# Attention pooling followed by SoLU on one core: six one-bank tiles for the first batch, nine early x buffers, output weights spread after pooling

## The chip, the cores and the metric

The kernel runs on one NeuronCore of one Trainium2 chip. The metric is the device time of one execution in microseconds, lower is better. The engines are called as the profile calls them: PE is TensorE (PEld its weight load), DVE is VectorE, ACT is ScalarE, POOL is GpSimd, and SP is SyncE, which here issues every DMA. PSUM has 8 banks; one bank holds 512 fp32 values per partition.

## The reference

```python
def mab(q, kv):                                   # scale = 1/sqrt(128)
    s = scale * (q @ kv.transpose(0, 2, 1))
    s = s - s.max(-1, keepdims=True)
    a = np.exp(s)
    a /= a.sum(-1, keepdims=True) + 1e-09
    return a @ kv
h = mab(I, x)          # x: 4 batches of 12608 tokens, 128 wide; I: 32 inducing rows
x = mab(x, h)          # 50432 tokens of 128
...
h = x @ w_in                                      # 128 -> 1024
solu = h * softmax(h)
ln = (solu - mean) / sqrt(var + 1e-06) * g_ln     # over 1024
out = ln @ w_out                                  # 1024 -> 128
```

All of it is fp32. The two weight matrices arrive as 64-bit floats and are turned to fp32 on the chip.

## The kernel before, in words

A batch has 99 tiles of up to 128 tokens (396 in all). The work on a batch has three parts.

- **Pooling, `p1(b, k)`**: nine blocks of up to 12 tiles. A block of x is loaded, each tile is turned by PE (L561) into a PSUM bank, ACT copies it to SBUF (L547), the turned block is stored in DRAM (`xd`, L571), PE makes the scores against the inducing rows (L589), DVE their maximum (L605, L609, with a PE product L614 that shares it between partitions, L623, L630), ACT the exponentials (L639), DVE transposes them (L659), PE multiplies them with x (L665), and DVE adds that to a running sum (L681). After the ninth block `combine` divides (L707 to L712), turns (L714) and copies the pooled rows (`h4`, L716), and multiplies them with `w_in` (L726, copied by ACT in L728).
- **Attention weights, `p2(b, j)`**: for 4, 8 or 12 tiles the turned block comes back from `xd` (L753), PE makes scores against the pooled rows (L768), and DVE, POOL and ACT make the softmax weights (L775 to L795); PE turns these (L804) and ACT copies them (L812).
- **Each tile, `main` and `soft`**: PE multiplies the turned weights with `h4 @ w_in` into the one `h` tile of two banks (L902), DVE reads it out, scaled and with its extreme (L940), into a buffer of the lock `HN`; ACT takes the exponential into a buffer of the lock `EU` (L950), POOL multiplies the two (L954), ACT sums the squares (L965), and DVE transposes in 32x32 blocks into a buffer `vt` that holds four tiles, a group (L978). PE then multiplies the group with the output weights `wc` (L1023) as two streams: stream 0 uses rows 0 to 63 of the array and the tile `op0`, stream 1 rows 64 to 127 and `op1`, 32 steps each. A step is called a beat here. L902 takes one half of the rows, so a beat of the other stream can run beside it. DVE or ACT copies the results (L1045), POOL and ACT normalise (`finish`, L1066 to L1102), SP stores them.

Pooling of batch b+1 runs among the tiles of batch b. For batch 0 there is nothing to run beside: this early phase borrows buffers that later have another use. x comes into `EARLY_X` (five pieces of the buffer `spare` and one `xn`), the turned x into pieces of `vt`, PSUM banks from the two halves of each `op` tile, two `h_e` banks, `pb` and `tr`. `handover` and `handover_op` give them to their later locks when batch 0 is pooled.

The weights are converted by `rounded`: a load (L405), integer operations on DVE (L410 to L419, L428), a copy on ACT (L421) and six multiplications and additions of half a matrix on POOL (L424 to L431). `weights_in` does that for `w_in`; `weights_out` for `w_out`, and then scales by `g_ln` on ACT (L453), subtracts the mean over the 1024 (PE L464, DVE L469) and spreads the result over `wc` with 16 DMAs (L481). No L1023 runs before all 16 have landed (`wc_ready`). While `rounded` runs, the five `eu` buffers and two `hn` buffers serve it.

The order of the instructions on every engine is made at build time by `Planner`. It keeps a clock for each engine, takes the engine whose next operation can start first, and on it, among the operations ready within `SLACK` of that, the one of smallest priority number. Costs, latencies (`AFTER`) and priorities (`PR_*`, `LATE`, `WOUT`) are constants. On the chip each engine then works its list in order. When PE's clock would stand for over `FILL` ns, the planner puts in transposes of the identity (L488). `SWITCH` is what it adds where PE goes from one kind of work to another, and `EAGER` by how much a beat may be planned ahead of its data.

## Time and profile before

| | us |
|---|---|
| median of 3 runs | 1289.62 (1284.67 to 1293.36) |
| the profiled execution | 1285.68 |
| its span | 1283.9 |
| granted PE clock, mean | 0.992 |

The span runs from the first to the last instruction; 1.8 us lie around it. Batch 0's pooled rows are copied (L716) at 52.4, the first tile is multiplied (L902) at 56.4, the first L1023 starts at 80.2, the last POOL multiplication (L954) ends at 1260.3 and the last L1023 at about 1274. Each PE product of fp32 stands in the profile as two records, a transpose as one. A beat of both streams (two products on each half of the rows) is eight records.

| tiles of L954 | from to us | us a tile | PE busy | DVE | ACT | POOL |
|---|---|---|---|---|---|---|
| 1 to 33 | 60.2 to 163.4 | 3.13 | 100.9 of 103 | 92.5 | 92.1 | 90.6 |
| 199 to 231 | 677.5 to 778.0 | 3.04 | 99.3 of 101 | 92.5 | 92.9 | 91.2 |
| 364 to 396 | 1171.7 to 1260.3 | 2.69 | 87.5 of 88 | 82.5 | 85.4 | 86.3 |

The last three rows of such a table (from 987 us on, when batch 3 is pooled) have no pooling beside the tiles. Busy PE is modelled from pipelined products, so a share near 100% doesn't say that it never waits.

### The profile page before, as it was taken

How to read it: one execution, taken by the hardware profiler on the slowest of the kernel's cores; microseconds unless marked ns; L12 is line 12 of the kernel's file. 1: busy time of each engine (PE TensorE's matmuls, PEld its weight loads, DVE VectorE, ACT ScalarE, POOL GpSimd, SP SyncE). 2: the span in 40 equal slices, each digit the busy share in tenths (PEclk: the TensorE clock that was granted, in tenths of full speed). 3: DMA queues.
4: the chain of work that ended last, by engine and by line, in shares of the span. 5: the costliest groups of instructions: out<-in, count | busy, mean ns of one | idle time of the engine just before them, and what ended most of it. 6: DMA issues, size and time to landing. Idle time of an engine off the chain costs nothing.

```text
span 1283.9 us, 75837 instructions
## 1 busy us (share of the span) xinstructions
PE 1246.2 (97%) x34221; PEld 1120.8 (87%) x34221; DVE 1140.8 (89%) x1825; ACT 1140.1 (89%) x2418; POOL 1104.2 (86%) x981
## 2 busy tenths in 40 slices
PE   8899999999999999999999999999999999999996
PEld 6689888889888888889888998888989999999996
DVE  5589989999898989999888999899999999999993
ACT  5489999999889989999789999989988999999993
POOL 2388988889889988988888997978889999999994
PEclk9999999999999999999899999999999999999998
DMA  9652333331232233332133134233021211111111
GB/s 361 188 164 70 111 103 94 93 111 43 77 117 60 78 102 119 103 109 74 28 102 94 43 103 138 91 101 102 21 82 54 58 55 53 54 38 43 29 29 41
DMA packets 118149, 113.46 MB, mean 88 GB/s; under 512 B 76577, under 2 KB 83777, under 8 KB 117697
## 3 DMA queue, kind: packets, MB, share of 16 engines
q1 hardware_dynamic: 117824, 108.62, 27.6%
q8 instruction: 267, 4.37, 1.4%
q14 instruction: 58, 0.47, 0.1%
HBM read 54.30 MB, written 52.18 MB: 83 GB/s over the span
## 4 chain that ended last, share of the span: by engine, by line
PE 70%; DVE 3%; ACT 2%; issue 1%; POOL 1%; POOLq 0%; DVEq 0%; ACTq 0%
PE op L1023 46%; PE h L902 15%; PE tr L561 2%; PE tr L804 2%; PE tr L768 1%; PE pb L665 1%; PE pb L589 1%; ACT sq L965 1%; DVE spare L940 1%; DVE vt L978 1%; ACT eu L950 1%; POOL eu L954 1%; PE pb L726 0%; DVE hn L940 0%; PE pb L614 0%
## 5 line engine op out<-in xcount | busy, mean ns | idle before, releaser
L1023 PE MATMUL op<-wc,vt 32*128 32x129 f32 x25600 | 1007.7, 275 | 12.5 <-issue 8.4
L1023 PEld LDWEIGHTS op<-wc,vt 32*128 32x128 f32 x25600 | 945.4, 185 | 54.3 <-issue 39.8
L902 PE MATMUL h<-hs,aT 32*128 32x128 f32 x6336 | 442.8, 277 | 3.2 <-DVE spare L940 1.2
L902 PEld LDWEIGHTS h<-hs,aT 32*128 32x128 f32 x6336 | 387.9, 187 | 32.1 <-DVE spare L940 6.2
L954 POOL TENSOR_TENSOR eu<-spare,eu 128x1024 f32<-128x1024 f32 x144 | 341.2, 2376 | 33.8 <-ACT eu L950 33.4
L954 POOL TENSOR_TENSOR eu<-hn,eu 128x1024 f32<-128x1024 f32 x140 | 331.8, 2376 | 25.1 <-ACT eu L950 24.3
L978 DVE STREAM_TRANSPOSE vt<-eu 128x1024 f32<-128x1024 f32 x284 | 349.2, 1233 | 1.1 <-POOL eu L954 0.9
L965 ACT ACTIVATE sq<-eu 128x1024 bf16<-128x1024 f32 x284 | 298.9, 1053 | 17.2 <-POOL eu L954 13.7
L940 DVE TENSOR_SCALAR_CACHE_REDUCE hn<-h,rn 128x1024 f32<-128x1024 f32 x198 | 252.1, 1273 | 38.8 <-PE h L902 30.6
L940 DVE TENSOR_SCALAR_CACHE_REDUCE spare<-h,rn 128x1024 f32<-128x1024 f32 x198 | 251.8, 1272 | 37.2 <-PE h L902 28.2
L950 ACT ACTIVATE eu<-hn,nm 128x1024 f32<-128x1024 f32 x140 | 160.3, 1145 | 19.9 <-DVE hn L940 19.0
L950 ACT ACTIVATE eu<-spare,nm 128x1024 f32<-128x1024 f32 x144 | 164.9, 1145 | 10.7 <-DVE spare L940 10.5
L954 POOL TENSOR_TENSOR spare<-hn,spare 128x1024 f32<-128x1024 f32 x58 | 137.5, 2374 | 15.6 <-ACT spare L950 15.5
L954 POOL TENSOR_TENSOR spare<-spare 128x1024 f32<-128x1024 f32 x54 | 128.0, 2373 | 16.9 <-ACT spare L950 16.4
L978 DVE STREAM_TRANSPOSE vt<-spare 128x1024 f32<-128x1024 f32 x112 | 138.2, 1235 | 0.0
L965 ACT ACTIVATE sq<-spare 128x1024 bf16<-128x1024 f32 x112 | 117.7, 1051 | 9.3 <-POOL spare L954 8.3
L1100 ACT ACTIVATE os<-spare,fin 128x128 f32<-128x128 f32 (+1 forms) x276 | 86.9, 391 | 1.5 <-POOL fin L1085 1.2
L950 ACT ACTIVATE spare<-hn,nm 128x1024 f32<-128x1024 f32 x58 | 66.4, 1145 | 6.7 <-DVE hn L940 6.4
L1045 DVE COPY spare<-op 128x258 f32<-128x258 f32 (+1 forms) x123 | 50.2, 416 | 24.6 <-PE op L1023 23.6
L950 ACT ACTIVATE spare<-spare,nm 128x1024 f32<-128x1024 f32 x54 | 61.9, 1146 | 6.5 <-DVE spare L940 6.5
L965 ACT ACTIVATION_READ_ACCUMULATOR sq<-eu 128x1 f32 x284 | 54.2, 191 | 0.0
L561 PE MATMUL tr<-ident,xn 128*128 128x128 f32 x297 | 48.8, 287 | 0.4 <-DMA xn<-in_x_dram 0.4
(180 smaller groups left out, 1028.0 us busy)
## 6 DMA issues: line engine op xcount, KB each, us to landing
out_dram<-os SPq DMA_DIRECT2D x96, 256.0 KB, 2.4
xT<-xd SPq DMA_DIRECT2D x27, 768.0 KB, 4.6
xn<-in_x_dram SPq DMA_DIRECT2D x22, 768.0 KB, 5.4
xd<-xT SPq DMA_DIRECT2D x21, 768.0 KB, 4.3
dl<-dd SPq DMA_DIRECT2D x396, 1.0 KB, 2.4
xd<-vt SPq DMA_DIRECT2D x7, 768.0 KB, 10.6
spare<-in_x_dram SPq DMA_DIRECT2D x5, 768.0 KB, 10.3
xT<-xd SPq DMA_DIRECT2D x5, 512.0 KB, 4.2
```

The costliest lines, as they stand in the source:

```text
L561: nc.tensor.transpose(out=tr[:, (s - c0) * P : (s - c0 + 1) * P], in_=xn[:, s, :], identity=ident)
L589: nc.tensor.matmul(sc[g * M : (g + 1) * M, : nn * M], lhsT=indT, rhs=xT[:, :nn, g * M : (g + 1) * M], start=True, stop=True)
L804: nc.tensor.transpose(out=tr[:h, (q - q0) * P : (q - q0 + 1) * P], in_=a4[:, q * P : q * P + h], identity=ident)
L902: nc.tensor.matmul(hp[:, cols], lhsT=aT[rows, i // 2, :], rhs=hs[rows, cols], start=True, stop=True)
L940: lambda: nc.vector.tensor_scalar(out=hn, in0=hp, scalar1=rn, scalar2=None, op0=ALU.mult, op1=ALU.min, accum_out=nm),
L950: "ACT", 1133, lambda: nc.scalar.activation(e, hn, AF.Exp, bias=nm, scale=-1.0, accum_out=G["S"][:, s : s + 1]), d, rel, srel,
L954: d = yield Op("POOL", 2330, lambda: nc.gpsimd.tensor_tensor(out=e, in0=hn, in1=e, op=ALU.mult), de, prio=t + PR_MU)
L965: "ACT", 1040, lambda: nc.scalar.activation(sq, e, AF.Square, scale=1.0 / 32.0, accum_out=G["qe"][:, s, 0:1]), d,
L978: lambda: nc.vector.transpose(out=G["vtb"][:, : n * FF].rearrange("p (j s t) -> p j s t", j=M, s=n)[:, :, s, :], in_=e.rearrange("p (a f) ...
L1023: nc.tensor.matmul(op[:rows, a - 2 * w, : C + 1], lhsT=vt[q, k, :], rhs=wc[q, k, :], start=(k == 0), stop=(k == JB - 1))
L1045: return lambda: eng(F["raw"][:rows, i0 : i0 + 2, :], op[:rows, :, : C + 1])
L1100: nc.scalar.activation(os[:rows, q, :], raw[:, q, :], AF.Copy, scale=y[:, i0 + q : i0 + q + 1])
```

## The change

The early phase and the constants of the planner are changed; what is computed stays the same.

- The early phase has six PSUM tiles of one bank each (`bank_e`) instead of four halves of `op` tiles and two `h_e` tiles: three for the turns, three (with `pb`) for scores and pooling. The `op` tiles are made afterwards, with `h`, in the space of the six. `handover_op` is gone, and `p2` of batch 0 uses the bank `tr` alone.
- x comes into nine buffers instead of six: two pieces of `wc` come first, then the five of `spare`, then both `xn`. The buffers for the exponentials move to `wc` and the two `os`.
- Since `wc` is borrowed, the column of ones (L474, now behind the pooled blocks) and the 16 spreads wait until batch 0 is pooled. `w_in`'s load goes from priority -18.5 to -10.5, `w_out`'s conversion from -13.5 to -10.5, the steps behind it (`LATE`) from -13 to -9, `combine` of batch 0 from -12 to -28. The mean over 1024 uses the bank `pb` instead of `tr`.
- After the early phase `HN` has one buffer more and `EU` one less. `EAGER` goes from 60 to 0; early PE work is planned without `SWITCH`.
- `SLACK` goes from 0 to 100 on ACT, from 300 to 100 on DVE and from 0 to 200 on POOL; `PR_MU` (POOL's multiplication) from -1 to -2, `PR_TU` (DVE's transpose) from 3 to 4.

New line numbers are within four of the old ones: L902 is L904 in the changed kernel, L940 L942, L954 L956, L1023 L1025, L481 L482.

```diff
-EAGER = 60
+EAGER = 0
-HN_MORE = 3
+HN_MORE = 4
-LATE = -13
-ON_EARLY = 3
+LATE = -9
-PR_MU = -1
+PR_MU = -2
-PR_TU = 3
+PR_TU = 4
-SLACK = {"PE": 100, "ACT": 0, "DVE": 300, "POOL": 0, "SP": 0}
+SLACK = {"PE": 100, "ACT": 100, "DVE": 100, "POOL": 200, "SP": 0}
-WOUT = -13.5
+WOUT = -10.5
+WIN = -10.5
...
-    op_b = [buf([P, 2, 512], f"op{w}", where=psum) for w in range(2)]
-    op_e = [o[:, i, :] for o in op_b for i in range(2)]
-    early_h = tc.tile_pool(name="h_early", bufs=1, space=PSUM, side="right")
-    where = early_h.__enter__()
-    h_e = [buf([P, 512], f"h_e{i}", where=where) for i in range(2)]
+    bank_pool = tc.tile_pool(name="early", bufs=1, space=PSUM, side="right")
+    where = bank_pool.__enter__()
+    bank_e = [buf([P, 512], f"bank_e{i}", where=where) for i in range(6)]
...
-        o = yield Op("POOL", 200, lambda: nc.gpsimd.memset(wc[:, :, C : C + 1], 1.0))
...
-        mp, rel = yield TRB
+        mp, rel = yield PB
...
+        for k in range(NP):
+            yield p1_done[0][k]
+        o = yield Op("POOL", 200, lambda: nc.gpsimd.memset(wc[:, :, C : C + 1], 1.0), [d for e in p1_done[0] for d in e.after])
+        o_end = [o]
...
-                    lambda: nc.sync.dma_start(rows[a * M : (a + 1) * M, :, q, :C], wg[q * M : (q + 1) * M]), d, issue=600, prio=LATE,
+                    lambda: nc.sync.dma_start(rows[a * M : (a + 1) * M, :, q, :C], wg[q * M : (q + 1) * M]), d, o, issue=600, prio=LATE,
...
-    EARLY_X = Lock([spare[:, i * each : (i + 1) * each].rearrange("p (s c) -> p s c", c=C) for i in range(SPARES * FF // each)] + xn_b[:1])
+    wc_flat = wc.rearrange("p j d -> p (j d)")
+    EARLY_X = Lock([f[:, i * each : (i + 1) * each].rearrange("p (s c) -> p s c", c=C) for f, n in ((wc_flat, 2), (spare, SPARES * FF // each)) for i in range(n)] + xn_b)
...
-    EARLY_TR = Lock(op_e[:3])
-    EARLY_PB = Lock([*h_e, pb_b, op_e[3]])
+    EARLY_TR = Lock(bank_e[:3])
+    EARLY_PB = Lock([*bank_e[3:], pb_b])
...
-            spawn(half(slice(k * 512, (k + 1) * 512)), PRIO_P1(b, NP - 1))
+            spawn(half(slice(k * 512, (k + 1) * 512)), PRIO_P1(b, NP - 1) if b else -28)
...
-        bank = EARLY_TR if b == 0 and j < ON_EARLY else TRB
+        bank = TRB
...
+        bank_pool.__exit__(None, None, None)
+        late = pool("late", 1, PSUM, side="right")
+        give(H, buf([P, FF], "h", where=late), *done)
+        for w in range(2):
+            give(OP[w], buf([P, 2, 512], f"op{w}", where=late), *done)
```

What the built lists say of it, at the three places of which the prediction speaks. First POOL, from the attention weights of tile group 0 to the multiplications of the first tiles (`s_*` and `a_*` are the scores and weights of p2; `hn_83` and `hn_85` with 512 columns are halves of `w_out`; rows of 1024 columns are tiles). Before:

```order
L424 TENSOR_TENSOR hn_83<-hn_83,eu 128x512 x2
L426 TENSOR_TENSOR hn_83<-hn_83,eu 128x512 x2
L431 TENSOR_TENSOR hn_83<-hn_83,eu 128x512 x2
L455 MEMSET wc 128x32
L780 TENSOR_TENSOR s_0_88<-s_0_88,mx_89 128x128
L788 COPY a_94<-a_94 128x4x32
L954 TENSOR_TENSOR eu<-hn_81,eu 128x1024
```

and changed:

```order
L782 TENSOR_TENSOR s_0_90<-s_0_90,mx_91 128x128
L790 COPY a_96<-a_96 128x4x32
L423 TENSOR_TENSOR hn_85<-hn_85,eu 128x512
L782 TENSOR_TENSOR s_1_93<-s_1_93,mx_94 128x256
L423 TENSOR_TENSOR hn_85<-hn_85,eu 128x512
L790 COPY a_96<-a_96 128x8x32
L425 TENSOR_TENSOR hn_85<-hn_85,eu 128x512 x2
L956 TENSOR_TENSOR spare<-hn_83,spare 128x1024
L782 TENSOR_TENSOR s_0_90<-s_0_90,mx_91 128x384
L430 TENSOR_TENSOR hn_85<-hn_85,eu 128x512
L790 COPY a_96<-a_96 128x12x32
L430 TENSOR_TENSOR hn_85<-hn_85,eu 128x512
```

The six halves of `w_out` stood ahead of the first attention weights of batch 0 and now stand between them and the tiles.

Second SP, the issues between the last store of turned x and the first loads of batch 1. Before:

```order
L571 DMA xd<-xT 128x896
L450 DMA g_sb<-in_moe_g_ln_dram 128x8x1
L481 DMA wc<-hn_83 32x8x128 x2
L753 DMA xT_87<-xd 128x1024
L481 DMA wc<-hn_83 32x8x128 x9
L753 DMA xT_87<-xd 128x1536
L481 DMA wc<-hn_83 32x8x128 x5
```

and changed:

```order
L573 DMA xd<-xT 128x896
L755 DMA xT_89<-xd 128x1024
L356 DMA xn_70<-in_x_dram 128x3x512
L755 DMA xT_89<-xd 128x1536 x2
L449 DMA g_sb<-in_moe_g_ln_dram 128x8x1
L755 DMA xT_89<-xd 128x1536
L482 DMA wc<-hn_85 32x8x128 x12
L1001 DMA dd_107<-qe_105 128x8
L482 DMA wc<-hn_85 32x8x128 x4
```

The spreads stood ahead of the second and third load for p2 and now stand behind five of them.

Third PE, the rows up to the first beat. Before, seven tiles are multiplied ahead of it, the last four rows of the way being:

```order
L804 MATMUL op_73<-ident,a_94 128x128 x4
L804 MATMUL op_72<-ident,a_94 128x128 x2
L902 MATMUL h<-hs_124,aT_97 128x128 x8
L561 MATMUL tr<-ident,xn_70 128x128 x4
L1023 MATMUL op_72<-wc,vt 128x129 x2
```

and changed, where they are twelve:

```order
L904 MATMUL h<-hs_126,aT_99 128x128 x8
L563 MATMUL tr<-ident,xn_70 128x128 x4
L489 MATMUL pb<-ident 128x128 x11
L904 MATMUL h<-hs_126,aT_99 128x128 x8
L563 MATMUL tr<-ident,xn_70 128x128 x4
L904 MATMUL h<-hs_126,aT_99 128x128 x8
L591 MATMUL pb<-xT,indT 32x384 x4
L904 MATMUL h<-hs_126,aT_99 128x128 x8
L1025 MATMUL op_637<-wc,vt 128x129 x4
```

Five more tiles stand ahead of the first beat. Over the whole list, counted in the same way, the beats from there to the end are 4187 before and 4195 changed (half-filled ones counted whole), POOL's scalings of the output, L1096 and now L1098, are 31 and 43 (ACT's, L1100 and now L1102, four to a group, 276 and 228), and the copies L1045/L1047 are 123 on DVE and 77 on ACT before, 101 and 99 changed.

More of the change, by code (lines that the diff above doesn't have):

```diff
@@ L311, in set_attention_then_solu_kernel @@
     EW = Lock()
-    OS = Lock(bufs(2, [P, GS, C], "os"))
+    os_b = bufs(2, [P, GS, C], "os")
+    OS = Lock()
     ST = Lock([
@@ L439, in weights_in @@
     def weights_in():
-        g = yield from rounded(w_in_sb, w_in.bitcast(U32), conv, None, conv_free, -18.5)
+        g = yield from rounded(w_in_sb, w_in.bitcast(U32), conv, None, conv_free, WIN)
         plan.set(w_in_ready, g)
@@ L473, in weights_out @@
         )
-        give(TRB, mp, d)
+        give(PB, mp, d)
+        for k in range(NP):
+            yield p1_done[0][k]
+        o = yield Op("POOL", 200, lambda: nc.gpsimd.memset(wc[:, :, C : C + 1], 1.0), [d for e in p1_done[0] for d in e.after])
+        o_end = [o]
         rows = wc.rearrange("p (k q) d -> p k q d", q=4)
@@ L561, in turn4 @@
                     nc.tensor.transpose(out=tr[:, (s - c0) * P : (s - c0 + 1) * P], in_=xn[:, s, :], identity=ident)
-            d = yield Op("PE", SWITCH + 108.7 * (c1 - c0), turn4, [d for d, at in xd if at < c1], trel, prio=None if early else RUSH)
+            d = yield Op("PE", (0 if early else SWITCH) + 108.7 * (c1 - c0), turn4, [d for d, at in xd if at < c1], trel, prio=None if early else RUSH)
             spawn(copy(c0, c1, tr, d), PRIO_P1(b, k))
@@ L591, in scores @@
                 )
-        d = yield Op("PE", SWITCH + n * 60, scores, ready, rel, ind_ready.after)
+        d = yield Op("PE", (0 if early else SWITCH) + n * 60, scores, ready, rel, ind_ready.after)
         def free_xT():
@@ L613, in p1 @@
         )
-        d = yield Op("PE", SWITCH + 110, lambda: nc.tensor.matmul(mq, lhsT=fold2, rhs=v["mdiag"], start=True, stop=True), d)
+        d = yield Op("PE", (80 if early else SWITCH) + 110, lambda: nc.tensor.matmul(mq, lhsT=fold2, rhs=v["mdiag"], start=True, stop=True), d)
         first = k == 0
@@ L1139, in set_attention_then_solu_kernel @@
                 starts.setdefault(NT * (b - 1) + int(P1_FROM + P1_STEP * k), []).append((p1(b, k), PRIO_P1(b, k)))
-        starts.setdefault(max(0, NT * (b - 1)), []).append((combine(b), PRIO_P1(b, NP - 1)))
+        starts.setdefault(max(0, NT * (b - 1)), []).append((combine(b), PRIO_P1(b, NP - 1) if b else -28))
         for j in range(len(at_groups[b])):
@@ L1149, in handover @@
             done += d
+        d = yield hw_ready[0]
+        done += d
+        bank_pool.__exit__(None, None, None)
[3 more added lines that the diff above has]
+            give(OP[w], buf([P, 2, 512], f"op{w}", where=late), *done)
+        give(PB, pb_b, *done)
+        for k in range(NP):
             d = yield xd_done[(0, k)]
             done += d
-        d = yield hw_ready[0]
-        done += d
-        early_h.__exit__(None, None, None)
-        give(H, buf([P, FF], "h", where=pool("h", 1, PSUM, side="right")), *done)
-        give(PB, pb_b, *done)
         wide = 4 * FG * (C + 1)
@@ L1166, in handover @@
         give(XT, xT_b, *done)
+        for o in os_b:
+            give(OS, o, *done)
         give(EW, ew_b, *done)
@@ L1169, in handover @@
             give(XN, a, *done)
-    def handover_op():
-        done = []
-        for k in range(NP):
-            d = yield p1_done[0][k]
-            done += d
-        for j in range(ON_EARLY):
-            d = yield aT_of[(0, j)]["all"]
-            done += d
-        for w in range(2):
-            give(OP[w], op_b[w], *done)
     def handover_tr():
@@ L1187, in set_attention_then_solu_kernel @@
     spawn(handover_tr(), -100)
-    spawn(handover_op(), 0)
     spawn(points(), -40)
```

5 lines of the change are left out of this document (2 added, 3 removed).

## Prediction

> **What bounds the kernel now.** I read the page's busy shares, its chain of waits and its groups first, then PE's timeline in the steady part, then all engines' timelines of the first 90 us.
>
> ```profile
> PE 1246.2 (97%) x34221; PEld 1120.8 (87%) x34221; DVE 1140.8 (89%) x1825; ACT 1140.1 (89%) x2418; POOL 1104.2 (86%) x981
> PE 70%; DVE 3%; ACT 2%; issue 1%; POOL 1%; POOLq 0%; DVEq 0%; ACTq 0%
> 602.12 2.08 PE L1023 MATMUL op<-wc,vt 32*128 32x129 f32 x68
> 604.02 0.28 PE L902 MATMUL h<-hs,aT 32*128 32x128 f32 x2
> ```
>
> PE stands on 70% of the chain that ended last, and the other three are busy for 86 to 89%: PE sets the pace, with little room behind it. The two timeline rows give the price of a beat: 68 records start in 604.02 - 602.12 = 1.90 us, so eight take 0.224 us. The 4187 beats behind the first L1023 are 938 us; the rest of that stretch is pooling and attention weights on PE, the turns between kinds of work, and waits.
>
> The early phase, by its marks:
>
> ```profile
> 8.06 1.53 PE L561 MATMUL op<-ident,spare 128*128 128x128 f32 x12
> ...
> 16.52 1.51 PE L561 MATMUL op<-ident,spare 128*128 128x128 f32 x12
> 17.96 0.85 PE L589 MATMUL pb<-vt,indT 128*32 128x384 f32 x8
> 18.74 0.66 PE L561 MATMUL op<-ident,spare 128*128 128x128 f32 x4
> 19.65 0.86 PE L665 MATMUL h_e<-spare,xn 128*32 128x128 f32 x24 [0.26 <-ACT vt L547]
> ...
> 42.36 0.57 PE L589 MATMUL h_e<-xT,indT 128*32 128x224 f32 x8 [0.69 <-ACT xT L547]
> 43.30 2.19 PE L488 MATMUL tr<-ident 128*128 128x128 f32 x18
> 45.55 2.16 PE L488 MATMUL tr<-ident 128*128 128x128 f32 x18
> 20.00:30.00 10.00, 9.26 (x129) 6.20 (x121) 6.88 (x28) 6.80 (x17) 7.45 (x6) 1.00 1.04 398
> 52.40 0.28 DVE L716 COPY h<-h_e 128x128 f32<-128x128 f32 x1
> 56.35 1.16 PE L902 MATMUL h<-hs,aT 32*128 32x128 f32 x16 [0.46 <-ACT aT L812]
> 80.19 1.50 PE L1023 MATMUL op<-wc,vt 32*128 32x129 f32 x42
> ```
>
> Turning a block of 12 tiles takes PE 1.44 us and its scores 0.78; with the sums against x (L665, 0.8 without its overlap) and the small product, about 0.3, a block costs 3.3 us, eight and a quarter blocks 27 us. PE turns from 8.06 us on, which makes 35 us, yet the pooled rows are copied at 52.4. In between stand fillers (x18 twice near the end) while DVE, ACT and the x still to come are waited for; the stretch from 20 to 30 us (busy PE, PEld, DVE, ACT, POOL, then granted clock, DMA share and GB/s) has the DMA engines full at 398 GB/s. From the pooled rows it takes 4 us to the first tile and 28 to the first L1023.
>
> **The change, part by part.** *Pooling earlier.* All x of batch 0 (6.46 MB) is now issued ahead of everything else: at 398 GB/s 16 us, so it has landed by about 20, and PE can go through its blocks without a wait: 8 + 27 = 35 us. Behind the last scores come the chains of the last blocks; before, 42.36 (the last L589) to 52.40 is 10.0 us, of which 3.1 are `w_out`'s mean and subtraction, which are gone from there. But `w_in`'s conversion now sits in the middle of DVE's list of the early phase. I take 46 us for the copy of the pooled rows, between 42 (35 + 10.0 - 3.1) and 52.4 (nothing gained), and 52 for the first tile: 4 as before plus 2, because ACT's copy for it now stands behind the copy of `w_out`, which waits for DVE's first operation on it.
>
> *The output weights later.* Their chain, each link from a row of before:
>
> ```profile
> 31.15 0.72 DVE L410 TENSOR_SCALAR eu<-eu 128x1024 uint32<-128x1024 uint32 x1 [0.46 <-DMA eu<-in_moe_w_out_dram]
> 34.64 1.22 DVE L415 SCALAR_TENSOR_TENSOR eu<-eu 128x1024 uint32<-128x1024 uint32 x1
> 39.07 2.51 POOL L424 TENSOR_TENSOR hn<-hn,eu 128x512 f32<-128x512 f32 x2 [1.00 <-ACT hn L421]
> 47.51 2.45 ACT L453 ACTIVATE hn<-hn,g_sb 128x128 f32<-128x128 f32 x8
> 49.10 2.05 PE L464 MATMUL tr<-hn,ones_mean 128*128 128x128 f32 x16
> 51.26 1.22 DVE L469 TENSOR_TENSOR hn<-tr,hn 128x1024 f32<-128x1024 f32 x1 [1.37 <-PE tr L464]
> 52.51 1.43 SPq L481 DMA_DIRECT2D wc<-hn  x2
> 54.63 5.92 SPq L481 DMA_DIRECT2D wc<-hn  x9
> 61.25 3.40 SPq L481 DMA_DIRECT2D wc<-hn  x5
> wc<-hn SPq DMA_DIRECT2D x16, 128.0 KB, 4.7
> ```
>
> DVE four operations of 0.72 and two of 1.22, 5.3; POOL three pairs of 2.51, 7.5; ACT 2.45, PE 2.0, DVE 1.2, SP 10.75, landing 4.7: 34 us. In the changed list it starts behind the first reciprocal of p2, some 3.5 us behind the pooled rows, at 49.5. Alone it would end at 83.5; that is the lower end. But POOL's six halves stand between p2's operations and the first tile's multiplication, two of L780 and two of L788 (2.5 us) and one L954 (2.4), and one collision is added:
>
> ```profile
> L780 POOL TENSOR_TENSOR s<-s,mx 128x384 f32<-128x384 f32 (+3 forms) x37 | 28.3, 764 | 13.7 <-DVE mx L777 13.7
> L788 POOL COPY a<-a 128x384 f32<-128x384 f32 (+3 forms) x37 | 17.6, 475 | 4.3 <-ACT a L787 4.2
> L954 POOL TENSOR_TENSOR eu<-spare,eu 128x1024 f32<-128x1024 f32 x144 | 341.2, 2376 | 33.8 <-ACT eu L950 33.4
> 49.60 0.29 DVE L712 TENSOR_SCALAR accn<-acc,small 128x128 f32<-128x128 f32 x1
> 633.42 2.33 DVE L712 TENSOR_SCALAR accn<-acc,small 128x128 f32<-128x128 f32 x1
> 633.33 2.35 POOL L954 TENSOR_TENSOR eu<-hn,eu 128x1024 f32<-128x1024 f32 x1 [0.66 <-ACT eu L950]
> ```
>
> The same small operation of DVE takes 0.29 us beside an idle POOL and 2.33 where POOL had begun a multiplication 0.09 us earlier; both end at 635.68. DVE's L427 (the last operation of the conversion, of the same kind) waits for exactly the POOL operation behind which L956 of the first tile stands, so it starts just after that and stands for some 2.3 us, with the second tile's reading, p2's maximum and the two last halves queued behind it. 83.5 + 2.5 + 2.4 + 2.3 = 90.7, of which the shorter first p2 blocks give back some; I take 90 for the first beat, and 94 for the upper end, where ACT's squares and the `dd` issue among the spreads also hold it. So the first beat comes 90 - 80.2 = 9.8 us later (3 to 14).
>
> [...]
>
> *What PE has to do from there.* Twelve tiles are multiplied by then instead of seven, but the beats that follow are 4195 instead of 4187: +1.8 us. Four turns of tiles, a block of scores and one of p2's stand ahead of the first beat instead of behind it: -1.8. The lists hold the same work otherwise, so a later first beat is a later end where PE is the bound. What comes back: three groups lie ready at 90, and PE has no data to wait for in the first tiles. I put 4 us on that, between 0 and 10 (five tiles of lead at about 2 us of beats that need not wait).
>
> *Balance between the engines.* These rows carry it:
>
> ```profile
> L1096 POOL TENSOR_TENSOR os<-spare,fin 128x512 f32<-128x512 f32 (+1 forms) x31 | 32.3, 1043 | 0.3
> L1045 DVE COPY spare<-op 128x258 f32<-128x258 f32 (+1 forms) x123 | 50.2, 416 | 24.6 <-PE op L1023 23.6
> L940 DVE TENSOR_SCALAR_CACHE_REDUCE hn<-h,rn 128x1024 f32<-128x1024 f32 x198 | 252.1, 1273 | 38.8 <-PE h L902 30.6 <-ACT eu L950 3.9 <-ACT fin L1076 1.3
> 677.00:778.00 101.00, 99.32 (x2791) 90.24 (x2794) 92.47 (x139) 92.89 (x194) 91.17 (x86) 1.00 0.28 84
> 1172.00:1260.00 88.00, 87.50 (x2630) 84.72 (x2632) 82.51 (x106) 85.44 (x183) 86.32 (x73) 1.00 0.12 32
> ```
>
> DVE loses 22 copies of 0.42, 9.2 us, on the engine that PE's next `h` waits for; I count 4 of it, since DVE waits for PE at L940 more than PE for DVE. POOL gains 12 scalings of 1.04, 12.5 us. In the middle it has room (91.2 of 101 busy), at the end none (86.3 of 88); three of the twelve lie in the last 99 tiles: +3.
>
> *The rest.* One more `HN` and one less `EU` buffer, the new slacks, priorities and `EAGER` change which of two ready operations goes first, hundreds of times. No row prices that. PE's 1194 us from 80.2 to the end of its last row
>
> ```profile
> 1261.83 12.25 PE L1023 MATMUL op<-wc,vt 32*128 32x129 f32 x382
> ```
>
> at 1274.1 hold 938 of beats and, by the prices above, about 135 of pooling and attention products; the 121 that remain are turns between kinds and waits. An eighth of these either way is 15 us; I take 0. The six banks of their own cost nothing in themselves: what they change is which early instruction waits, and that is in the 46.
>
> The sum: +9.8 + 1.8 - 1.8 - 4 - 4 + 3 = +4.8. On the profiled execution's 1285.7 that is 1290.5; the median of the runs is 3.9 higher, which would make 1294.4. I forecast 1292.
>
> **Rivals.**
> *PE is not the bound but the chain of a tile through DVE, ACT and POOL.* Then the late first beat is made up for (twelve tiles are ready), the first tile's 56.4 - 52 = 4.4 stays a gain and DVE's copies count in full: 1285.7 - 4.4 - 9.2 = 1272, and with an order that gains the whole 15, 1257. For it speaks that DVE, ACT and POOL together leave PE no room in the last third; against it PE's 70% of the chain.
> *POOL becomes the bound.* It takes the twelve scalings on top of a first beat that is late: 1285.7 + 9.8 + 12.5 = 1308. It decides once POOL's idle time in the middle, 10 of 101 us, falls to the 2 of 88 that it has at the end. Against it: the scalings are spread over all batches, one for every 33 tiles.
> *The early phase is no earlier.* The DMA engines run at their limit until 40 us in either list, and `w_in` now lands behind all x, so its conversion may hold the first tile: pooled rows at 52 as now, the first beat at 96, and 1285.7 + 16 - 5 = 1297. Speaks for it the share of 1.04 above; against it that x needs less than half of these 40 us.
> [...]
>
> ```profile
> 60.00:70.00 10.00, 10.00 (x85) 8.41 (x84) 5.10 (x9) 5.01 (x11) 6.99 (x5) 0.73 1.19 224
> ```
>
> **How the numbers follow.** The forecast's case has 0.40, the early phase that is no earlier 0.10: both end within 1%, which is about what a measurement of this kernel can tell from no change (its three runs span 0.7%). The tile chain as the bound has 0.27 and ends faster by over 1%; POOL as the bound has 0.23 and ends slower by over 1%. The likeliest case's own range is 1278 to 1303 (first beat 3 to 14 later, lead 0 to 10, half of the 15 for the order); with the two others, and about a tenth left out on each side, 1264 to 1312.
>
> **What would show it.** Right: the copy of the pooled rows (L718) near 46, the first L904 near 52, the first L1025 near 90 with twelve L904 ahead of it, DVE's second L427 at over 2 us, the time from the first to the last L1025 within 10 us of 1194. Wrong: a first L1025 before 84, or a stretch of L1025 shorter by more than 15 us, which would say that the order or DVE's relief decides and not PE's count of beats; POOL above 95% from 300 to 1000 us would say the second rival.

## The result

The changed kernel takes 1297.38 us in the median of 14 runs (1292.23 to 1305.58), the kernel before 1288.89 (14 runs, 1284.67 to 1293.36): a ratio of 1.0075, 95% interval 1.0057 to 1.0093. That is 9.7 us longer by the ratio (7.3 to 12.0) and 8.5 by the medians. The profiled execution took 1292.23 us, the shortest of the 14, with a span of 1290.4, against 1285.68 and 1283.9 before.

The page's busy shares and granted clock of the changed kernel (most lines stand two further down than before: L902 is L904 here, L1023 is L1025, L954 is L956):

```profile
PE 1254.5 (97%) x34255; PEld 1129.8 (88%) x34255; DVE 1126.9 (87%) x1806; ACT 1133.3 (88%) x2392; POOL 1116.4 (87%) x990
...
PEclk9889999999999999999999999999999999999998
```

DVE lost 14 us of work (9.2 had been counted) and POOL gained 12 (12.5 counted); PE's share is as it was. The two groups that moved, busy time and mean ns behind the bar:

```profile
L1098 POOL TENSOR_TENSOR os<-spare,fin 128x512 f32<-128x512 f32 (+1 forms) x43 | 44.8, 1042 | 2.7
L1047 DVE COPY spare<-op 128x258 f32<-128x258 f32 (+1 forms) x101 | 41.3, 416 | 25.2 <-PE op L1025 24.3
```

The early phase, PE's timeline first (last scores of pooling, second score product of p2, the turn of p2's first weights, first tile, a later tile and the mean of `w_out`, first beat):

```profile
30.63 0.57 PE L591 MATMUL bank_e<-xT,indT 128*32 128x224 f32 x8 [0.21 <-ACT xT L549]
...
49.27 0.64 PE L770 MATMUL tr<-xT,h 128*32 128x256 f32 x8
52.02 0.41 PE L806 MATMUL tr<-ident,a 128*128 128x128 f32 x2 [0.86 <-DVE s L777]
52.89 1.16 PE L904 MATMUL h<-hs,aT 32*128 32x128 f32 x16 [0.46 <-ACT aT L814]
...
69.86 2.08 PE L904 MATMUL h<-hs,aT 32*128 32x128 f32 x16
71.87 3.44 PE L461 MATMUL pb<-hn,ones_mean 128*128 128x128 f32 x16
...
90.17 0.38 PE L1025 MATMUL op<-wc,vt 32*128 32x129 f32 x2
```

DVE in the same stretch: the pooled rows, the rounding of `w_out` with the transpose of p2's second scores (L777) behind it, the second tile's reading (L942), and the last operation of the rounding (L427).

```profile
43.71 0.29 DVE L718 COPY h<-bank_e 128x128 f32<-128x128 f32 x1 [0.58 <-PE bank_e L716]
...
47.25 0.66 DVE L409 TENSOR_SCALAR eu<-eu 128x1024 uint32<-128x1024 uint32 x1
...
50.29 1.22 DVE L415 SCALAR_TENSOR_TENSOR eu<-eu 128x1024 uint32<-128x1024 uint32 x1
51.43 0.44 DVE L777 STREAM_TRANSPOSE s<-tr 128x256 f32<-128x256 f32 x1
...
58.49 1.28 DVE L942 TENSOR_SCALAR_CACHE_REDUCE spare<-h,rn 128x1024 f32<-128x1024 f32 x1 [2.77 <-PE h L904]
...
60.27 1.06 DVE L427 TENSOR_SCALAR eu<-hn 128x1024 f32<-128x1024 int32 x1
```

ACT's copy of `w_out`, POOL's first multiplication beside that L427, and SP's spreads:

```profile
47.95 1.07 ACT L420 ACTIVATE hn<-eu 128x1024 f32<-128x1024 int32 x1 [0.82 <-DVE eu L409]
```

```profile
58.42 2.35 POOL L956 TENSOR_TENSOR spare<-hn,spare 128x1024 f32<-128x1024 f32 x1
```

```profile
76.64 8.67 SPq L482 DMA_DIRECT2D wc<-hn  x12
85.42 0.54 SPq L1001 DMA_DIRECT2D dd<-qe  x1
86.00 2.57 SPq L482 DMA_DIRECT2D wc<-hn  x4
```

Batch 0's scores end 11.7 us earlier than before (30.63 against 42.36), its pooled rows 8.7 (43.71 against 52.40), the first tile 3.5 (52.89 against 56.35), and the first beat comes 10.0 us later (90.17 against 80.19). The early phase gains, and the gain is used up on the way to the first beat. The tiles themselves are not late by then: the twelfth is multiplied at 89.61 in the changed kernel and at 93.06 before. To see where it grows, the start of POOL's 34th multiplication, the time from there to its 298th, and from there to the span's end, in us (one profiled execution each; the experiments stand here too):

| kernel | 34th | to the 298th | to the end |
|---|---|---|---|
| before | 163.4 | 823.9 | 296.6 |
| changed | 168.8 | 822.8 | 298.8 |
| E1 before, detour | 174.2 | 826.9 | 296.3 |
| E2 changed, detour | 176.3 | 827.0 | 299.0 |
| E3 changed, no rounding | 166.4 | 830.0 | 298.6 |
| E4 changed, conversions early | 168.7 | 824.1 | 301.6 |
| E5 changed, no fillers | 168.8 | 824.3 | 298.9 |
| E6 E4 without fillers | 167.2 | 827.2 | 311.1 |
| E7 changed, old constants | 169.4 | 828.3 | 297.3 |
| E8 before, new constants | 171.1 | 825.0 | 303.3 |
| E9 changed, scalings to ACT | 171.4 | 827.6 | 301.5 |
| E10 before, scalings to ACT | 165.1 | 824.7 | 302.1 |
| E11 before, beat 226 | 164.7 | 827.1 | 296.4 |
| E12 changed, early and old constants | 168.4 | 830.1 | 297.7 |

The changed list stands in E2, E3 and E5 too, with edits at its start or end; these four differ by up to 7 us in the middle column and by 0.4 in the last. How much of the 7 is scatter and how much comes from the edits is not told apart. Of the 6.5 us between the two spans, 5.4 stand ahead of the 34th tile, 2.2 behind the 298th, and the -1.1 between them is too small to read.

### The profile page after: what moved, and what is told of

The parts are those of the page before. It is cut to its first block, busy times and chain, and to the rows that moved or that the text cites. A ratio compares the mean times of both kernels' runs of the same rounds, so it can differ in the third digit from the quotient of the medians.

```text
span 1290.4 us, 75904 instructions
## 1 busy us (share of the span) xinstructions
PE 1254.5 (97%) x34255; PEld 1129.8 (88%) x34255; DVE 1126.9 (87%) x1806; ACT 1133.3 (88%) x2392; POOL 1116.4 (87%) x990
## 5 line engine op out<-in xcount | busy, mean ns | idle before, releaser
L1025 PE MATMUL op<-wc,vt 32*128 32x129 f32 (+1 forms) x25600 | 999.3, 274 | 7.7 <-issue 4.9
L1025 PEld LDWEIGHTS op<-wc,vt 32*128 32x128 f32 (+1 forms) x25600 | 935.9, 184 | 45.3 <-issue 34.2
L956 POOL TENSOR_TENSOR eu<-spare,eu 128x1024 f32<-128x1024 f32 x189 | 447.1, 2373 | 31.5 <-ACT eu L952 31.2
L904 PE MATMUL h<-hs,aT 32*128 32x128 f32 x6336 | 443.4, 277 | 6.5 <-DVE spare L942 4.7
L904 PEld LDWEIGHTS h<-hs,aT 32*128 32x128 f32 x6336 | 387.0, 187 | 39.9 <-DVE spare L942 12.1
L980 DVE STREAM_TRANSPOSE vt<-eu 128x1024 f32<-128x1024 f32 x329 | 404.6, 1234 | 14.4 <-POOL eu L956 13.8
L967 ACT ACTIVATE sq<-eu 128x1024 bf16<-128x1024 f32 x329 | 345.6, 1050 | 30.3 <-POOL eu L956 25.9
L956 POOL TENSOR_TENSOR eu<-hn,eu 128x1024 f32<-128x1024 f32 x140 | 331.4, 2372 | 15.8 <-ACT eu L952 15.2
L942 DVE TENSOR_SCALAR_CACHE_REDUCE spare<-h,rn 128x1024 f32<-128x1024 f32 x228 | 289.8, 1271 | 51.3 <-PE h L904 43.7
L942 DVE TENSOR_SCALAR_CACHE_REDUCE hn<-h,rn 128x1024 f32<-128x1024 f32 x168 | 213.1, 1268 | 29.4 <-PE h L904 24.8
L952 ACT ACTIVATE eu<-spare,nm 128x1024 f32<-128x1024 f32 x189 | 216.2, 1144 | 14.3 <-DVE spare L942 13.6
L956 POOL TENSOR_TENSOR spare<-spare 128x1024 f32<-128x1024 f32 x39 | 92.5, 2372 | 7.9 <-ACT spare L952 7.9
L980 DVE STREAM_TRANSPOSE vt<-spare 128x1024 f32<-128x1024 f32 x67 | 82.7, 1235 | 3.4 <-POOL spare L956 3.1
L967 ACT ACTIVATE sq<-spare 128x1024 bf16<-128x1024 f32 x67 | 70.4, 1050 | 5.5 <-POOL spare L956 4.0
L1102 ACT ACTIVATE os<-spare,fin 128x128 f32<-128x128 f32 (+1 forms) x228 | 72.4, 389 | 1.5 <-POOL fin L1087 1.2
L956 POOL TENSOR_TENSOR spare<-hn,spare 128x1024 f32<-128x1024 f32 x28 | 66.5, 2375 | 6.8 <-ACT spare L952 6.8
L1047 DVE COPY spare<-op 128x258 f32<-128x258 f32 (+1 forms) x101 | 41.3, 416 | 25.2 <-PE op L1025 24.3
L1047 ACT COPY spare<-op 128x258 f32<-128x258 f32 (+1 forms) x99 | 35.6, 368 | 21.0 <-PE op L1025 18.4
L549 ACT COPY xT<-tr 128x512 f32<-128x512 f32 (+1 forms) x75 | 42.8, 571 | 6.5 <-PE tr L563 4.4
```

What stands on the lines that cost most here:

```text
L549: lambda: nc.scalar.copy(xT[:, c0:c1, :], tr[:, : (c1 - c0) * P].rearrange("p (s t) -> p s t", t=P)),
L904: nc.tensor.matmul(hp[:, cols], lhsT=aT[rows, i // 2, :], rhs=hs[rows, cols], start=True, stop=True)
L942: lambda: nc.vector.tensor_scalar(out=hn, in0=hp, scalar1=rn, scalar2=None, op0=ALU.mult, op1=ALU.min, accum_out=nm),
L952: "ACT", 1133, lambda: nc.scalar.activation(e, hn, AF.Exp, bias=nm, scale=-1.0, accum_out=G["S"][:, s : s + 1]), d, rel, srel,
L956: d = yield Op("POOL", 2330, lambda: nc.gpsimd.tensor_tensor(out=e, in0=hn, in1=e, op=ALU.mult), de, prio=t + PR_MU)
L967: "ACT", 1040, lambda: nc.scalar.activation(sq, e, AF.Square, scale=1.0 / 32.0, accum_out=G["qe"][:, s, 0:1]), d,
```

## The experiments

Theory 1 is the prediction's: the late first beat passes to the end. Theory 2: the tiles that are ready make up for it, and the loss lies elsewhere. The others are named as they came up.

**E1 and E2: the first beat later.** In both kernels the output weights make a detour on SP; all orders stay.

```diff
+        trip = xd_pool.tile([P, FF], F32, name="trip")
+        def put():
+            if (a, q) == (2, 3):      # E2: (3, 0)
+                nc.sync.dma_start(trip, wg2)
+                nc.sync.dma_start(wg2, trip)
+            nc.sync.dma_start(rows[a * M : (a + 1) * M, :, q, :C], wg[q * M : (q + 1) * M])
```

> The kernel before, with every engine's order left as it is; only SP, before the last five of the sixteen spreads of the output weights, sends them once to DRAM and back (two transfers of 512 KB, which change no value). The first multiplication by the output weights (the first beat, 80.2 us in the kernel before) should come some 9 to 11 us later. Theory 1 (PE's count of beats sets the end, and a first beat that is late stays late): the time rises by 6 to 11 us, ratio 1.005 to 1.009. Theory 2 (the tiles that are ready by then make up for it, and the changed kernel's loss lies elsewhere): at most 2 us, ratio under 1.002.

> The changed kernel with the same detour of the output weights through DRAM, before the last four spreads, all orders as they are. First beat at 99 to 101 us in place of 90.2. Theory 1: another 6 to 11 us on the changed kernel, so 1303 to 1308, ratio to the kernel before 1.011 to 1.016. Theory 2: 1297 to 1299, ratio 1.0065 to 1.009.

SP's rows in E1 and the first beat (L1031 is L1023 of the kernel before):

```profile
61.14 0.44 SPq L480 DMA_DIRECT2D trip<-hn  x1
69.23 0.32 SPq L481 DMA_DIRECT2D hn<-trip  x1
72.92 3.24 SPq L482 DMA_DIRECT2D wc<-hn  x5
```

```profile
89.75 1.50 PE L1031 MATMUL op<-wc,vt 32*128 32x129 f32 x42
```

E1: 9.6 us later, ratio 1.0066 (1.0040 to 1.0092), that is 8.5 us (5.2 to 11.9); the table shows it ahead of the 34th tile, with nothing given back behind. But the detour did not move the first beat alone. SP works its list in order, so the load of x for batch 1 (L357) that stands behind the spreads was issued at 76.21 in place of 64.70, and PE's next turn waited for it, ahead of the tiles. These are the two rows, and 70 to 80 us before and in E1:

```profile
76.21 0.61 SPq L357 DMA_DIRECT2D xn<-in_x_dram  x1
81.30 1.12 PE L569 MATMUL tr<-ident,xn 128*128 128x128 f32 x4 [10.63 <-DMA xn<-in_x_dram]
```

```profile
70.00:80.00 10.00, 9.38 (x102) 7.76 (x100) 9.46 (x18) 7.74 (x16) 7.60 (x8) 1.00 0.49 167
```

```profile
70.00:80.00 10.00, 0.68 (x13) 0.48 (x10) 3.28 (x4) 0.00 (x0) 1.93 (x4) 0.74 0.75 171
```

Each of the four engines stood for 10.6 to 12.6 us in one piece there, which the changed kernel's do not. The weights were not what PE waited for: by the trace the last spread landed at 78.3, 11.5 us ahead of E1's first beat, and in the kernel before at 71.7, 8.5 us ahead. So the expected first beat came, but by luck, on another path. E1 shows that a stop of all four engines at the start is paid at the end. It does not test a first beat that is late while the tiles go on.

E2: first beat at 94.97, 4.8 later than in the changed kernel (9 to 11 had been expected), ratio 1.0136 (1.0099 to 1.0172), that is 7.9 us above the changed kernel's 1.0075 (some 3 to 13 by the two intervals). The 4.8 are not the detour's: the twelfth tile, which stands ahead of the beat, is itself 4.8 late (94.41 against 89.61), and this execution was granted 0.50 of the clock from 70 to 80 us and 0.67 from 80 to 90, the changed one 0.76 and 1.00. What the detour adds stands behind: PE waits for the last spreads,

```profile
96.73 3.60 PE L1033 MATMUL op<-wc,vt 32*128 32x129 f32 x50 [0.22 <-DMA wc<-hn]
```

and batch 1's next load of x is issued at 95.33 in place of 88.62. (L1033 is L1025 of the changed kernel. Its first products start before all 16 spreads have landed: the last one lands at 97.3 here and at 90.9 in the changed kernel, by the trace.)

The two profiles without a detour answer theory 2 in part. Counted over the 25600 records of L1023 and L1025, the changed kernel is 10.0 us behind at the first record, 5.7 at the 2000th, 6.1 at the 8000th, 1.8 at the 20000th and 6.5 at the last. In E3 and E5, whose lists begin as the changed one does, 6.3 falls to 3.2 and 10.4 to 5.9 by the 2000th. So in these lists some 4 us come back early, as the prediction had it, and the rest does not. That the ready tiles are the reason is not tested, and in E7, another list, 8.0 grows to 13.0 by then. What comes later goes up and down by several us, of which one execution each says little.

**E3: the first beat earlier, order held.** The rounding of `w_out` is left out on DVE and POOL.

```diff
-        ts, stt = nc.vector.tensor_scalar, nc.vector.scalar_tensor_tensor
-        gt, gs = nc.gpsimd.tensor_tensor, nc.gpsimd.tensor_scalar
+        skip = lambda **_: None
+        ts, stt, gt = (nc.vector.tensor_scalar, nc.vector.scalar_tensor_tensor, nc.gpsimd.tensor_tensor) if not after else (skip,) * 3
```

> The changed kernel without the seven DVE and six POOL operations that round the output weights (left out: that rounding, so these weights hold other numbers), all remaining orders as they are, every load, copy, gain, mean and spread kept. The first beat should come at 80 to 84 us in place of 90.2, when PE has issued the twelve tiles ahead of it. Theory 1: the time falls by about as much, 6 to 9 us, to about 1290, ratio to the kernel before 0.999 to 1.003. Theory 2: it stays at 1296 to 1298, ratio 1.006 to 1.009.

```profile
86.46 0.58 PE L1025 MATMUL op<-wc,vt 32*128 32x129 f32 x2
```

The first beat moved less than expected, 3.7 us, since the mean of `w_out` keeps its place in PE's list behind the tiles; the ratio fell to 1.0035 (1.0014 to 1.0055), 5.2 us below the changed kernel's (1.7 to 8.7 by the two intervals); by the mean times, 1295.8 against 1298.1, it is 2.3. This fits theory 1. But DVE and POOL also have less to do, and the tiles come earlier with the beat (the twelfth at 85.43 in place of 89.61), so no run here moves the first beat alone.

**E4: the conversions early again, list made anew.**

```diff
-LATE = -9
+LATE = -13
-WOUT = -10.5
-WIN = -10.5
+WOUT = -13.5
+WIN = -18.5
```

> The changed kernel with only the places of the two conversions put back (WIN -18.5, WOUT -13.5, LATE -13): six banks, nine x buffers, the new slacks and priorities stay. First beat near 80 us again, with fewer tiles ahead of it; the planner makes its list anew. Theory 1: 1288 to 1291, ratio 0.998 to 1.003, since the first beat is where it was. Theory 3 (the new constants of the steady part, slacks and priorities, cost the 8 us): 1296 to 1299, ratio 1.005 to 1.009.

```profile
81.13 2.10 PE L1025 MATMUL op<-wc,vt 32*128 32x129 f32 x32
```

The first beat is back within 1 us of the old one, and yet the ratio is 1.0059 (1.0039 to 1.0078). Theory 1 is not enough for this list: the table has it 5.3 us late at the 34th tile and 5.0 longer behind the 298th.

**E5 and E6: the fillers.** The new lists hold something that was not costed: PE's filler transposes late in the run, which the planner puts where it sees PE wait. The changed kernel has 45 behind 1100 us, E4 has 83 behind 200, the kernel before none. This is their row among the changed kernel's groups of the last 300 us, with no idle time ahead of them:

```profile
L489 PE MATMUL tr<-ident 128*128 128x128 f32 x45 | 5.8, 277 | 0.0
```

Theory 4: they cost their time. Both kernels run without them:

```diff
-                    self.fill(buf)
+                    if at < 200000:
+                        self.fill(buf)
```

> The changed kernel without the 45 filler transposes (L489) that stand in four places of PE's list behind 1100 us; every other instruction and order as it was. They write nothing that is read. Theory 4 (PE has no idle time there, so the fillers, 45 of 108 ns or 4.9 us, are paid in full and make up about half of the loss): 1292 to 1294, ratio to the kernel before 1.002 to 1.005; the last two stages of 33 tiles fall from 92.2 and 89.7 us to about 89.5 and 88.5. Theory 1 alone (the late first beat is the whole loss, the fillers stand in time that PE would have waited): 1296 to 1299, ratio 1.006 to 1.009.

> The changed kernel with the conversions put back to their early places (first beat 81.1 us) and without the 83 filler transposes behind 200 us that this list had. Theory 1 with theory 4 (late first beat and fillers together are the loss): both are gone here, 1287 to 1290, ratio 0.997 to 1.001. Theory 3 (something else in the new slacks and priorities costs 6 us or more): 1294 to 1297, ratio 1.004 to 1.006.

E5: 1.0084 (1.0060 to 1.0109), E6: 1.0101 (1.0072 to 1.0130). Theory 4 falls: without fillers E5 is no faster and E6 looks slower than E4, though their intervals meet. The last 99 tiles of the changed kernel and of E5 (busy time of PE, PEld, DVE, ACT, POOL, then clock, DMA share, GB/s):

```profile
991.60:1269.30 277.70, 273.82 (x8157) 260.67 (x8153) 250.73 (x339) 256.93 (x533) 269.32 (x235) 1.00 0.16 43
```

```profile
993.10:1270.50 277.40, 269.09 (x8100) 256.33 (x8095) 250.64 (x339) 257.32 (x533) 269.29 (x235) 0.99 0.16 43
```

PE has 4.7 us less to do, the stretch is 277.4 in place of 277.7: PE waits where the fillers stood. (E5's profile is the fastest of its twelve runs, so no more than this stretch is read from it.) So a row with no idle time ahead of it does not show that its work was on the path. The same stretch in E4 and E6:

```profile
992.80:1273.30 280.50, 278.11 (x8239) 264.81 (x8243) 253.21 (x344) 257.43 (x529) 271.98 (x239) 0.99 0.16 43
```

```profile
994.40:1284.60 290.20, 278.67 (x8177) 265.87 (x8181) 253.45 (x343) 257.09 (x528) 271.81 (x239) 0.96 0.16 41
```

DVE, ACT and POOL do the same work, PE has fewer records, and the granted clock is 0.96 in place of 0.99; the stretch is 9.7 us longer. This is E6's slowest run (1307.5 us; the mean of its six is 1303.5), so the usual difference is smaller.

**E7 and E8: the constants apart from the structure.** E7 puts the five old values into the changed kernel, E8 the five new ones into the kernel before.

```diff
-EAGER = 0
+EAGER = 60
-HN_MORE = 4
+HN_MORE = 3
-PR_MU = -2
+PR_MU = -1
-PR_TU = 4
+PR_TU = 3
-SLACK = {"PE": 100, "ACT": 100, "DVE": 100, "POOL": 200, "SP": 0}
+SLACK = {"PE": 100, "ACT": 0, "DVE": 300, "POOL": 0, "SP": 0}
```

> The changed kernel with EAGER, HN_MORE, PR_MU, PR_TU and SLACK of the kernel before: the early phase and the late output weights stay, the steady part is planned by the old rules; this list has no fillers behind the first beat. Theory 1 with theory 4: the late first beat stays, the fillers are gone, 1292 to 1295, ratio 1.002 to 1.006. Theory 1 alone: 1296 to 1299. Theory 3: 1287 to 1290, ratio 0.997 to 1.001.

> The kernel before with only EAGER, HN_MORE, PR_MU, PR_TU and SLACK of the changed one: early phase and output weights as before, first beat near 80 us; this list has 65 fillers (7.0 us) behind 200 us. Theory 1 with theory 4: the fillers alone, 1295 to 1299, ratio 1.004 to 1.008. Theory 1 alone: 1288 to 1291, ratio 0.998 to 1.002. Theory 3: 1296 or more whatever the fillers cost, with the loss in other stages than those that hold them.

The first beats, E7 and then E8:

```profile
88.15 0.58 PE L1025 MATMUL op<-wc,vt 32*128 32x129 f32 x2
```

```profile
79.83 1.94 PE L1023 MATMUL op<-wc,vt 32*128 32x129 f32 x58
```

E7: 1.0072 (1.0044 to 1.0099) with a first beat 8.0 us late; E8: 1.0080 (1.0055 to 1.0105) with one in its old place. The new structure with its late weights costs as much as the whole change, the new constants in the old structure do too (theory 3 holds for them), and the two together are no worse than either. E8 loses 7.7 us ahead of the 34th tile and 6.7 behind the 298th, where it has 14 POOL scalings in place of 9 (the changed kernel 12).

**E9 and E10: is POOL the bound at the end?** Theory 5: POOL, with 8.4 of 277.7 us idle in the last 99 tiles, sets their pace. Its scalings there go to ACT.

```diff
             def scaled():
+                if plan.now > 955000:     # E10: 943000
+                    return scaled_act()
...
```

> The changed kernel with the twelve POOL scalings of the outputs that stand behind its 297th tile given to ACT (same values, four operations of 0.32 us each in place of one of 1.05 on POOL), everything else in its order. Theory 5 (POOL, which has under 0.1 us of idle time per tile there, sets the pace of the last 99 tiles, and the change's three more scalings there are part of the loss): POOL loses 10.5 us in this stretch, ACT gains 12.6 of the 21 us that it had idle; the last three stages shrink from 277.6 us to 268 to 272, the time to 1288 to 1292, ratio to the kernel before 0.999 to 1.003. Theory 6 (no one engine paces it; the order of the lists does): within 2 us of the changed kernel, ratio 1.006 to 1.010.

> The kernel before with its nine scalings behind the 297th tile given to ACT in the same way. Theory 5: POOL loses 7.4 us of the last 99 tiles, ACT gains 8.8 of its 13.5 idle ones, so less comes of it than in the changed kernel: 1285 to 1288, ratio 0.996 to 0.999. Theory 6: no change or slower, since ACT has hardly more room than POOL, 1289 to 1294, ratio 1.000 to 1.004.

E9: 1.0098 (1.0071 to 1.0125); E10: 1.0026 (1.0012 to 1.0039). Both no faster, and E10 slower than the kernel before. The last 99 tiles of E9:

```profile
999.00:1278.60 279.60, 273.74 (x8113) 259.95 (x8113) 250.74 (x339) 266.86 (x573) 259.39 (x225) 1.00 0.16 43
```

POOL has 9.9 us less to do than in the changed kernel and ACT 9.9 more, and the stretch is 1.9 longer. Theory 5 falls as it was put. But ACT got what POOL lost, and stands at 266.9 of 279.6 us: the run does not show what less work on POOL alone would bring. E5 took 4.7 us of fillers from PE there for nothing.

**E11: a list made anew for no reason.** Theory 6: any new list loses against the old one.

```diff
-BEAT = 225
+BEAT = 226
```

> The kernel before, planned again with one number that means nothing for the machine: a beat's cost in the planner 226 ns instead of 225. Early phase and first beat stay (80 us), the order of the rest is shuffled a little. Theory 6 (a list made anew loses several us against the list of the kernel before, whatever was changed): 1296 to 1302, ratio 1.005 to 1.010, with the loss spread over the stages. Theories 1 and 5 alone: 1288 to 1292, ratio 0.999 to 1.002, as neither the first beat nor POOL's share at the end changes.

0.9994 (0.9977 to 1.0012): theory 6 falls as it was put, since this list loses nothing. It is one list, shuffled a little; how much of what E4, E7 and E8 lose belongs to the order that the planner happened to find for them stays open.

**E12: the six banks and nine x buffers alone.** E4's early conversions together with E7's old constants.

> The changed kernel with the conversions back in their early places and EAGER, HN_MORE, PR_MU, PR_TU and SLACK of the kernel before: what is left of the change are the six banks, the nine x buffers and the hand-over. First beat near 80 us, no fillers behind it. Theory 1 together with theory 3 (the late first beat costs 7 to 10 us, the new slacks and priorities cost as much by themselves, and nothing else does): both are gone, 1288 to 1292, ratio 0.999 to 1.003. Theory 7 (the six banks themselves cost it: batch 0's attention products all in one bank, and x buffers that are other tiles' storage): 1295 to 1300, ratio 1.004 to 1.008.

1.0039 (1.0023 to 1.0055), between the two: 5.0 us (3.0 to 7.1). Its profile has the reason in PE's timeline and granted clock:

```profile
58.07 1.88 PE L904 MATMUL h<-hs,aT 32*128 32x128 f32 x16 [0.46 <-ACT aT L814]
59.88 3.46 PE L489 MATMUL pb<-ident 128*128 128x128 f32 x15
...
80.86 2.08 PE L904 MATMUL h<-hs,aT 32*128 32x128 f32 x16
...
85.58 0.58 PE L1025 MATMUL op<-wc,vt 32*128 32x129 f32 x2
```

```profile
60.00:70.00 10.00, 9.87 (x59) 7.42 (x59) 4.85 (x7) 3.62 (x7) 4.17 (x3) 0.50 1.25 182
70.00:80.00 10.00, 9.43 (x63) 7.62 (x67) 7.28 (x12) 8.33 (x16) 8.04 (x5) 0.50 0.38 95
```

Its spreads are issued from 56.72 on, 4.2 us behind the old ones. But PE was granted 0.50 of its clock from 60 to 80 us and 0.55 from 80 to 90, a tile's product takes 2.08 us in place of 1.16, and the first beat is 5.4 us late. Theory 7 is thus not shown: what is lost is about as much as the first beat is late, and the clock stretched the way there. This is the slowest of E12's twelve runs, with a mean clock of 0.983 where the twelve have 0.987; the others lost less of it.

**What the clock has to do with it.** The stretch from 40 to 100 us, in the order before, E11, changed, E7, E12:

```profile
40.00:100.00 60.00, 55.28 (x891) 45.27 (x891) 42.67 (x79) 40.23 (x87) 40.57 (x32) 0.94 0.55 137
```

```profile
40.00:100.00 60.00, 55.53 (x893) 45.48 (x892) 42.90 (x80) 40.58 (x88) 40.55 (x33) 0.94 0.54 138
```

```profile
40.00:100.00 60.00, 51.39 (x646) 41.63 (x645) 45.18 (x76) 37.88 (x79) 42.35 (x35) 0.91 0.49 130
```

```profile
40.00:100.00 60.00, 49.47 (x588) 37.70 (x592) 45.04 (x74) 38.25 (x80) 42.27 (x34) 0.80 0.53 136
```

```profile
40.00:100.00 60.00, 54.77 (x631) 43.35 (x633) 37.34 (x67) 33.44 (x70) 37.88 (x31) 0.74 0.51 119
```

The lists with a late first beat have 27 to 34% fewer records on PE here, and a lower clock. Each run lists its mean granted clock too. Within one kernel, a run whose clock is 0.001 lower is 0.98 us longer (least squares over the runs of all these kernels, each about its own mean; 1.14 for 82 runs of the kernel before alone), nearly the 1.29 us that 0.001 of the span is. Means by kernel, and what each time would be at the clock of the kernel before by this slope:

| kernel | first beat, us | ratio | clock | mean, us | at 0.992 |
|---|---|---|---|---|---|
| before | 80.2 | 1 | 0.9920 | 1290.1 | 1290.2 |
| E11 beat 226 | 79.8 | 0.9994 | 0.9938 | 1289.4 | 1291.1 |
| E12 early, old constants | 85.6 | 1.0039 | 0.9873 | 1295.0 | 1290.5 |
| E7 changed, old constants | 88.2 | 1.0072 | 0.9853 | 1299.7 | 1293.1 |
| changed | 90.2 | 1.0075 | 0.9887 | 1298.1 | 1294.9 |
| E5 changed, no fillers | 90.6 | 1.0084 | 0.9862 | 1300.5 | 1294.9 |
| E4 early | 81.1 | 1.0059 | 0.9907 | 1297.4 | 1296.1 |
| E6 early, no fillers | 79.4 | 1.0101 | 0.9853 | 1303.5 | 1297.0 |
| E8 before, new constants | 79.8 | 1.0080 | 0.9902 | 1300.9 | 1299.1 |
| E10 before, scalings to ACT | 82.0 | 1.0026 | 0.9928 | 1293.5 | 1294.4 |
| E9 changed, scalings to ACT | 91.1 | 1.0098 | 0.9888 | 1302.8 | 1299.7 |
| E3 changed, no rounding | 86.5 | 1.0035 | 0.9904 | 1295.8 | 1294.3 |
| E1 before, detour | 89.8 | 1.0066 | 0.9896 | 1298.1 | 1295.8 |
| E2 changed, detour | 95.0 | 1.0136 | 0.9855 | 1307.2 | 1300.9 |

By this working out some 3 of the 8.0 us between these means go with the clock, and 5 do not (the kernel before stands with the 82 runs beside the experiments). It is a correlation. For E5 and E6 only the fillers differ, and there both pairs come together once the clock is taken out: 1294.9 and 1294.9, 1296.1 and 1297.0. Nor is the clock shown to be a cause apart from the late start: E1, whose engines stood still, has 0.91 from 40 to 100 us too. By the slope E12 and E7 lose mostly clock, and the structure with the old constants would be within 3 us of the kernel before if PE were kept at its clock. That was not tried.

No list tried here beats the kernel before; E11 equals it.

## Why the prediction was right

The time came out in the case that was forecast (slower by less than 1%, with a first beat some 10 us later); 1297.4 is inside the case's own 1278 to 1303. Of the change itself the sum had half: +4.8, where 9.7 were measured by the ratio and 6.5 between the two profiled executions. And that the late first beat alone makes this loss is not shown: E4 and E8 lose as much without one. Step by step:

- *Pooled rows at 46:* 43.71; the scores ended at 30.6, earlier than the 35 that the block prices gave.
- *First tile at 52:* 52.89, but by luck: it comes 9.2 us behind the pooled rows, where 6 were counted, and these came 2.3 early. The reason given was not it either. ACT's copy of `w_out` was done at 49.0. The tile waited for the turn of p2's first weights (L806): with all of batch 0's products in the one bank `tr`, PE's second score product (49.27) had first to be read by DVE's L777, and that stood behind the rounding of `w_out` until 51.43. The step that moved `w_out` counted who waits on ACT's queue and not on DVE's.
- *First beat at 90, twelve tiles ahead:* 90.17, with errors in the sum that cancel. The chain of `w_out` began at 47.25 in place of 49.5 and took about that much longer. DVE's L427 was costed at 2.3 us and took 1.06: the second tile's L942 stood ahead of it, so that it began 1.85 us into POOL's multiplication. It ended 0.56 us behind that multiplication's end at 60.77 (the same operation takes 0.68 in E4, `w_in`'s takes 0.68 at 37.52 in this kernel, where POOL has no row beside it), so it did take longer beside the multiplication, but by 0.38 us where 2.3 had been added. Why it takes longer there is not shown. The rows from which L427's price came were also read a little off: the small operation there ended at 635.75, 0.07 us behind POOL's, not with it. In place of that wait, PE's mean began at 71.87 although ACT's scaling was done at 69.07, behind a tile of 2.08 us, and took 3.44 us against 2.05 before; 0.52 of the clock was granted from 70 to 75 us. The spreads took 11.9 us of SP in place of 10.75. At the end the beat stood behind the twelfth tile (89.61), which waited for DVE's reading of the one before it, as much as behind the spreads.
- *A late first beat is a late end, less 4 us:* the profiles agree with the 4, by the records of L1025 counted above (10.0 late at the first, 5.7 at the 2000th), though E7's list does not give it back. E1 (9.6 give 8.5) had no tiles ready, since all engines stood, and E3 (-3.7 give -5.2) moved more than the beat. The first-to-last stretch of L1025 is 1190 us against 1194, inside the 10 allowed.
- *DVE's 22 copies, -4:* they went as counted (123 to 101) and brought nothing that the runs show.
- *POOL's scalings at the end, +3:* twelve in place of nine stand there, and the stretch behind the 298th tile is 2.2 us longer; but E9 moved them from POOL to ACT without gain, so POOL's load is not shown as the reason.
- *The order, 0:* mis-sized. E8 shows that the five constants alone cost 10 us (7 to 14) in the old structure; in the new one, where E7 and the changed kernel are equal, they cost nothing that can be measured. With early conversions the pair is E4 and E12, 1.0059 and 1.0039, whose intervals overlap. Why E8's and E4's lists lose with an early first beat stays open: the table puts it ahead of the 34th tile and behind the 298th, in about equal parts. Their profiles have 0.91 and 0.89 of the clock from 40 to 100 us against 0.94, which over 60 us is 2 to 3 us and can be a part of the early one.
- *The clock, not in the sum:* leaving it out failed. The 0.73 in the prediction's last row, from 60 to 70 us, is of the kernel before; the changed one was granted 0.90 there, but 0.76 in place of 1.00 from 70 to 80. In all, the kernel before lost less of it: 0.94 from 40 to 100 us against 0.91, and 0.9920 against 0.9887 over all runs, about 3 us by the slope above. The median lies 5.4 us above the forecast.

The rivals: that the tile chain alone is the bound, with a gain, did not occur (the copies taken from DVE did not show); POOL as the bound did not show (POOL is busy for 623 of the 700 us from 300 to 1000 us, 89% and not 95%, and E9 and E10 gained nothing); the early phase was earlier, so the third falls too. But E5 took fillers from PE and E9 work from POOL in the last 99 tiles, and neither made them shorter. "PE sets the pace" was too simple for this stretch. What sets it there, with four engines at 87 to 97% and each with its list in a fixed order, was not found.
